# Attention beside a feed-forward network on one core: one feed-forward pair moved to between the value products and the second key tile's scores

## The chip, the cores and the metric

The kernel runs on one core of a Trainium2 chip. The metric is the device time of one execution in microseconds (us); less is better. TensorE (PE in the profile) multiplies matrices and writes to eight banks of accumulators (PSUM); its weight loads are listed apart as PEld. VectorE (DVE), ScalarE (ACT) and GpSimd (POOL) do the rest, and SyncE (SP) issues most transfers. The engines run side by side and wait for each other through semaphores.

## The reference

```python
xn = _layernorm(x)                          # x: [1, 2048, 512]
q, k, v = split(xn @ wqkv)                  # 32 heads of 16
p = _softmax(q @ k^T * 16 ** -0.5)          # full, over 2048 keys
s = (p @ v) @ wo
h = _silu(xn @ w_gate) * (xn @ w_up)        # 1792 hidden features
g = _silu(h @ w_down)
return x + s * g
```

All inputs are float32. One block of 2048 tokens goes through attention with 32 small heads and, beside it, through a gated feed-forward network; the second's result gates the first's.

## The kernel before

The kernel has a prologue of some 160 us (normalising, transposing, projecting to queries, keys and values, which go to memory in the layout that attention reads), an attention loop, and a short end for the last token block.

**Attention.** The heads are taken in 8 groups of 4 and the tokens in 4 query blocks of 512, which gives 32 units (`u`). Each unit runs over the 2048 keys in 8 steps of two key tiles of 128 (`kp`, and `i` = 0 or 1 in it), 256 steps in all. For a key tile TensorE makes four score matrices of 128 keys x 512 queries, one a head (line 811). The heads of a group sit in the two halves of the array's rows, so two of these matmuls form a pair and run beside each other. A pair fills one of two score tiles (`score[0]`, `score[1]`, `j` = 0 or 1) of two accumulator banks each, and one ScalarE instruction of 1024 columns takes the exponential of it into SBUF (line 813). Both key tiles of a step use the same two score tiles, so each pair of scores has to wait until the exponential of the pair two before it has read its tile.

Between the first and the second key tile's scores stand the value products of the step before (`values(prev)`, line 356): 16 matmuls of 17 columns (16 values and a column of ones that gives the sum), four beside each other in four strips of the array's columns. The order of a step on TensorE is thus: scores of key tile 0, value products of the previous step, scores of key tile 1, feed-forward work.

**Feed-forward work.** The network's matmuls, and the output projection behind them, are written as generators (`ffn`, `project_out`). Each `next` of one issues a pair: two matmuls that take the two halves of the contraction in the two halves of the array's rows, into `bankx` and `banky` (`both`, line 174). The precision of float32 is kept by splitting operands into a high and a low part, three products for each. A tile of the up projection (128 of the 1792 gate and up features for 512 tokens) has 24 pairs; a tile of the down projection has 24 or 18. When a tile's last pair is issued, ScalarE and VectorE empty the two banks; until then both belong to that tile. The generator yields the number of pairs that its tile still lacks, which the kernel before doesn't use. Some instructions hang on a pair's number: behind the 8th pair of an up-projection tile its down weights are fetched, behind the last one the tanh, the products and the splitting of the hidden features follow.

**Who gets how many.** `plan` writes the list `shares`, one entry a step: an up-projection tile is spread over three steps of 8 pairs, a down-projection tile of 24 over three of 8 or, every eighth, two of 12, one of 18 over two of 9, an output-projection tile is one step. `share()` at a step's end, behind the second key tile's scores, takes the next entry and calls `fill(n)`, which draws n pairs. The first steps are given some pairs by hand (`FIRST`). TensorE takes everything in the order in which it is written.

Of the kernel before, what the change touches and what calls it, by code (L numbers as in the profile page):

```python
# [50 lines left out]
def tile_block(ctx: ExitStack, tc: tile.TileContext, x, wqkv, wo, w_gate, w_up, w_down, out):  # L51
# [51 lines left out]
    def load_k(g, c, i=None):  # L103
        load_rows(kst[(g * NB + c) % RING if i is None else i],
                  k_d[:, g * 64:(g + 1) * 64, c * TB:(c + 1) * TB], KSLOT)

    def load_q(u, i=None):
        g, b = divmod(u, NB)
        load_rows(qst[u % 2 if i is None else i], q_d[:, g * 64:(g + 1) * 64, b * TB:(b + 1) * TB], QSLOT)

    def load_shift(u):
        for h in range(2):
            sp.dma_start(qst[u % 2][h * HALF:h * HALF + 2].bitcast(F32),
                         sh_d.rearrange("(s u) (j h t) -> u h s j t", s=2, j=2, h=2)[u, h])

    def load_v(g, c):
        sp.dma_start(vst[(g * NB + c) % RING], v_d[g][:, c * CT:(c + 1) * CT])
# [38 lines left out]
    def catch_up():  # L156
        while after:
            after.pop(0)()
# [131 lines left out]
    def out_steps():  # L290
        for b in range(NB - 1):
            if b not in stage and (len(queue) <= NB, 0 in stage and now > stage.get(0, now), ready[0] == DT)[b]:
                for c in range(DT - 1):
                    load_out(b, c)
                stage[b] = now
            if b in stage and b < 2 and (b, 1) not in stage and now > (u0 + b) * steps:
                load_out(b, DT - 1)
                stage[b, 1] = now
            if b in stage and (b, 2) not in stage and now > stage[b] and (b < 2 or len(queue) <= 2):
                splits.extend((b, c) for c in range(DT - 1))  # L300
                stage[b, 2] = now
                for t in range(0 if b else NT):
                    load_gates(t)
            if (b, 1) in stage and (b, 5) not in stage and now > stage[b, 1]:
                splits.insert(0 if not b else len(splits), (b, DT - 1))
                stage[b, 5] = now
        for _ in range(min(2, len(splits))):
            b, c = splits.pop(0)
            split_o(lhs[b, c], parts_o[b, c])
            ready[b] += 1  # L310
# [27 lines left out]
    def load_gate():  # L338
        last.extend(on[:3] + [one.tile([P, D], F32, tag="wdr", name="last")])
        for t in range(NT):  # L340
            r = rows[(NB - 1) * NT + t]
            sp.dma_start(gate[t], g_d[r])
            sp.dma_start(last[t], x[r])

    def gate_rest(t):
        dve.scalar_tensor_tensor(facc[:, t], facc[:, t], 0.5, gate[t], op0=ALU.mult, op1=ALU.mult)
        dve.tensor_add(facc[:, t], facc[:, t], last[t])


    def values(item):  # L350
        u, kp, probs = item
        v, a = vst[(u // NB * NB + kp * 2 // CT) % RING], acc[u % 2]
        for i in range(2):
            kt = 2 * kp + i
            for h in range(4):
                mm(a[h * 32:h * 32 + DH + 1], v[:, kt % CT, h * (DH + 1):(h + 1) * (DH + 1)],  # L356
                   probs[2 * i + h // 2][:, h % 2], start=kt == 0, stop=kt == KT - 1, skip_group_check=True)
# [35 lines left out]
    queue = [[None, ffn(b), NF * 3 * (DC + NT)] for b in range(NB)]  # L393
    queue += [[None, project_out(NB - 1, DT - 1), EARLY * 3 * (DT - 1)]]
    queue += [[b, project_out(b), NT * 3 * DT] for b in range(NB - 1)]
    total = sum(q[2] for q in queue)
    given = 0

    now = -1

    def fill(n):
        nonlocal given
        while n > 0 and not blocked():
            next(queue[0][1])
            queue[0][2] -= 1
            if not queue[0][2]:
                queue.pop(0)
            n -= 1
            given += 1
# [3 lines left out]
    shares = []  # L413
# [24 lines left out]
    def blocked():  # L438
        return not queue or queue[0][0] is not None and ready[queue[0][0]] < DT

    def share():
        if not blocked() and shares:
            fill(shares.pop(0))


    with ExitStack() as pro:
# [211 lines left out]
        for b in range(NB):  # L658
# [3 lines left out]
            for n, (make, i) in enumerate(slots):  # L662
# [56 lines left out]
                if not more and n == 9:  # L719
                    tops = pps.tile([P, 512], F32, tag="ps", name="tops")  # L720
                    nc.tensor.transpose(tops[0:1, :P], sm, ident)
                    dve.reduce_max(s4, tops[0:1, :P], axis=AX.X)
                    dve.tensor_scalar(s4, s4, 0.51, None, op0=ALU.mult)
                    dve.tensor_scalar(flag, s4, LIMIT, None, op0=ALU.is_le)
                    dve.tensor_scalar(sel[:, :NG * NB], row[:, :NG * NB], s4, None, op0=ALU.mult)
                    for h in range(2):
                        dve.tensor_copy(selq[:, h * HALF:h * HALF + 1], s4)
                    fill(3 * DC)
                    low, high = [pps.tile([P, 512], F32, tag="ps", name="low") for _ in range(2)]
                    mm(high[:2 * NG * NB, :8], sel, row[:, :8], start=True, stop=True, skip_group_check=True)  # L730
                    mm(low[:HALF + 2, :8], selq, row[:, :8], start=True, stop=True, skip_group_check=True)
                    act(shift, high[:2 * NG * NB, 0:1].to_broadcast([2 * NG * NB, 512]), AF.Copy, scale=-1.0)
                    for h in range(2):
                        two_rows = slice(h * HALF, h * HALF + 2)
                        act(qst[0][two_rows], low[two_rows, None, 0:1].to_broadcast([2, 2, 512]), AF.Copy, scale=-1.0)
                    for j in range(4):
                        pool.dma_start(sh_d[:, j * 512:(j + 1) * 512], shift.bitcast(F32))
                    fast = nc.values_load(flag, min_val=0, max_val=1)
# [58 lines left out]
    for u in range(units):  # L797
        g, b = divmod(u, NB)
        q = qst[u % 2]
        for kp in range(steps):  # L800
            now = u * steps + kp
            probs = []
            for i in range(2):
                kt = 2 * kp + i
                k, kc = kst[(g * NB + kt // CT) % RING], kt % CT
                if now == i == 0:
                    fill(FIRST[0])
                for j in range(2):
                    for h in range(2):
                        r = slice(h * HALF, h * HALF + NROW)  # L810
                        mm(score[j][:, h], k[r, j, kc * P:(kc + 1) * P], q[r, j], start=True, stop=True)  # L811
                    pr = ppool.tile([P, 2, TB], F32, tag="pr", name="pr")
                    exps.append(act(pr, score[j], AF.Exp, scale=0.25))  # L813
                    if i == 0 and j == 1 and now:
                        tc.add_manual_dep(exps[-1].ins, exps[-3].ins.name, settled, reason="order of the slots' writes")
                    probs.append(pr)
                    if now == i == 0 and j:
                        fill(FIRST[1])
                    elif (now, i, j) in ((0, 1, 0), (1, 0, 0)):
                        fill(FIRST[2 + now])  # L820
                if i == 0:
                    catch_up()
                if i == 0 and prev:
                    values(prev)
            old, prev = prev, (u, kp, probs)
            share()
            if old and old[1] == steps - 1:
                after.append(partial(finish, old[0]))
            if kp == 0:
                if u + 1 < units:  # L830
                    load_q(u + 1)
                    load_shift(u + 1)
            if g + 1 < NG and (b == 0 and kp == 0 or b == NB - 1 and kp in (2, 4, 6)):
                load_k(g + 1, kp // 2)
                load_v(g + 1, kp // 2)
            out_steps()
            if now == (units - 1) * steps + 1:
                load_gate()
            if 0 <= now - (units - 1) * steps - 4 < EARLY:
                gate_rest(now - (units - 1) * steps - 4)  # L840
# [79 lines left out]
```

## Time and profile before

| | before |
|---|---|
| time of 3 runs: median (lowest to highest) | 1437.24 us (1437.2 to 1437.76) |
| span of the profiled execution, first to last instruction | 1435.2 us |
| granted TensorE clock, mean | 1.000 |
| busy between 200 and 1200 us of the span (1000 us): TensorE, ScalarE, VectorE | 1000.0, 825.9, 337.1 us |
| DMA share of its engines between 200 and 400 us | 0.26 |

The timed runs include what lies around the span; the median is 2.0 us above it. A row of the profile reads: line of the code, engine, operation, what it writes <- what it reads, shape, how often, then busy time and mean duration, then the idle time of the engine ahead of it and who ended that. A row of the timeline begins with its start and its length in us, and "x2" means that two like instructions are merged in it. Two matmuls in different halves of the rows run beside each other and start within some nanoseconds, so a pair is one place in TensorE's time.

### The profile page before, as it was taken

To read this page: it belongs to the slowest core of one execution; us is meant where nothing else is said; L and a number is where in the kernel's file an instruction comes from. 1 tells how busy PE (TensorE), PEld (TensorE's weight loads), DVE (VectorE), ACT (ScalarE), POOL (GpSimd) and SP (SyncE) were. 2 spreads that over 40 slices of the span, in tenths; PEclk is the share of its full clock that TensorE was granted. 3 is DMA by queue.
4 is the path that set the end of the run, shared out by engine and by line. 5 is a ranking of instruction groups with operands and counts; after the bars stand their busy time and mean duration, and the time that the engine had idled before them with its cause. 6 is when DMAs were issued, how large, how long until landed. Compare 5 with 4: busy or idle time off the path is not lost.

```text
span 1435.2 us, 26816 instructions
## 1 busy us (share of the span) xinstructions
PE 1427.3 (99%) x11227; PEld 804.0 (56%) x11227; DVE 537.9 (37%) x899; ACT 1111.2 (77%) x1235; POOL 90.9 (6%) x104
## 2 busy tenths in 40 slices
PE   9999999999999999999999999999999999999998
PEld 7778655555555555555555555555555555555555
DVE  6543344112523343134323441243244422243665
ACT  6733688888888888778888888888888887888764
POOL 4200200000000000000000000000000000000154
PEclk9999999999999999999999999999999999999999
DMA  7778652032264321142553320342835210312553
GB/s 222 264 246 248 160 116 63 19 90 65 67 149 120 96 65 34 39 105 71 112 132 90 95 48 12 79 106 55 177 79 123 63 42 12 101 30 78 196 183 104
DMA packets 127524, 149.15 MB, mean 104 GB/s; under 512 B 12588, under 2 KB 79404, under 8 KB 126628
## 3 DMA queue, kind: packets, MB, share of 16 engines
q1 hardware_dynamic: 122196, 126.84, 34.5%
q0 software_dynamic: 4912, 20.12, 3.8%
q8 instruction: 91, 1.49, 0.5%
q10 hardware_dynamic: 288, 0.39, 0.1%
q14 instruction: 37, 0.30, 0.1%
HBM read 107.20 MB, written 40.11 MB: 103 GB/s over the span
## 4 chain that ended last, share of the span: by engine, by line
PE 89%; DVE 0%; DVEq 0%; issue 0%
PE acc L356 33%; PE bankx L174 31%; PE score L811 20%; PE banky L174 3%; PE acc L858 0%; PE banky L858 0%; PE score L858 0%; DVE y L865 0%; DVE y L871 0%; DVEq L916 0%
## 5 line engine op out<-in xcount | busy, mean ns | idle before, releaser
L813 ACT ACTIVATE pr<-score 128x1024 f32<-128x1024 f32 x1024 | 993.2, 1023 | 223.2 <-PE score L811 222.5
L356 PE MATMUL acc<-pr,vst 128*17 128x512 f32 x4096 | 489.2, 595 | 0.0
L811 PE MATMUL score<-qst,kst 50*128 50x512 f32 x2048 | 352.3, 421 | 0.0
L811 PEld LDWEIGHTS score<-qst,kst 50*128 50x128 f32 x2048 | 177.2, 184 | 263.8 <-ACT pr L813 227.9
L174 PE MATMUL bankx<-fx,guh 64*128 64x512 f32 x896 | 288.8, 392 | 0.1
L174 PE MATMUL banky<-fx,guh 64*128 64x512 f32 x896 | 288.7, 392 | 0.0
L356 PEld LDWEIGHTS acc<-pr,vst 128*17 128x17 f32 x4096 | 93.9, 96 | 234.4 <-issue 233.6
L204 DVE SCALAR_TENSOR_TENSOR ga<-th,bankx 128x512 f32<-128x512 f32 x56 | 38.5, 687 | 446.1 <-ACT th L203 446.1
L174 PEld LDWEIGHTS bankx<-fx,guh 64*128 64x128 f32 x896 | 165.7, 185 | 32.8 <-issue 0.9
L174 PE MATMUL banky<-fx,gul 64*128 64x512 f32 x448 | 175.3, 391 | 0.0
L174 PE MATMUL bankx<-fx,gul 64*128 64x512 f32 x448 | 175.3, 391 | 0.0
L174 PEld LDWEIGHTS banky<-fx,guh 64*128 64x128 f32 x896 | 165.6, 185 | 4.0
L174 PE MATMUL bankx<-wd,hh 64*128 64x512 f32 x672 | 166.7, 389 | 0.0
L174 PE MATMUL banky<-wd,hh 64*128 64x512 f32 x672 | 166.6, 388 | 0.0
L174 PEld LDWEIGHTS bankx<-wd,hh 64*128 64x128 f32 x672 | 124.0, 185 | 26.6
L174 PEld LDWEIGHTS banky<-wd,hh 64*128 64x128 f32 x672 | 124.0, 185 | 1.2
L174 PEld LDWEIGHTS bankx<-fx,gul 64*128 64x128 f32 x448 | 82.8, 185 | 17.0
L174 PEld LDWEIGHTS banky<-fx,gul 64*128 64x128 f32 x448 | 82.8, 185 | 2.0
L569 PE MATMUL ps<-xt,wh 128*128 128x512 f32 x256 | 80.6, 396 | 0.0
L222 DVE COPY facc<-bankx 128x512 f32<-128x512 f32 x16 | 11.1, 691 | 171.5 <-PE banky L174 171.5
L135 DVE TENSOR_TENSOR gul<-gur,guh 128x1024 fp32r<-128x1024 f32 x56 | 68.6, 1225 | 2.4 <-DVE guh L134 0.5
L379 POOL DMA_DIRECT2D o_d<-o x12 | 6.5, 545 | 756.5 <-DVE o L377 563.8
(158 smaller groups left out, 1060.5 us busy)
## 6 DMA issues: line engine op xcount, KB each, us to landing
gur<-in_B_w_gate_dram SPq DMA_DIRECT2D x56, 256.0 KB
gur<-in_B_w_up_dram SPq DMA_DIRECT2D x56, 256.0 KB
wdr<-in_B_w_down_dram SPq DMA_DIRECT2D x56, 256.0 KB
kst<-k_d SPq DMA_DIRECT2D x192, 64.0 KB
qst<-q_d SPq DMA_DIRECT2D x192, 64.0 KB
fx<-xt_d SPq DMA_DIRECT2D x24, 512.0 KB
q_d<-parts SPq DMA_DIRECT2D x16, 512.0 KB
k_d<-parts SPq DMA_DIRECT2D x16, 512.0 KB
```

The lines of the kernel that those rows point to most:

```text
L135: dve.tensor_sub(lo, raw, hi.bitcast(F32))
L174: mm(bank, lhs[h], rhs[h], start=start, stop=stop)
L204: dve.scalar_tensor_tensor(ga, th, 1.0, bankx, op0=ALU.add, op1=ALU.mult)
L222: dve.tensor_copy(facc[:, t], bankx)
L356: mm(a[h * 32:h * 32 + DH + 1], v[:, kt % CT, h * (DH + 1):(h + 1) * (DH + 1)], probs[2 * i + h // 2][:, h % 2], start=kt == 0, stop=kt == ...
L379: (pool if g < NG - 1 else sp).dma_start(o_d[g // 2, b], o2)
L569: mm(ps, w, a[:, c], start=n == 0, stop=n == 3 * DT - 1)
L811: mm(score[j][:, h], k[r, j, kc * P:(kc + 1) * P], q[r, j], start=True, stop=True)
L813: exps.append(act(pr, score[j], AF.Exp, scale=0.25))
```

## The change

`fill` keeps what the generator yields, in `left`: the number of pairs that the tile under way still lacks, 0 when a tile is complete. In the step loop, right behind the value products and so ahead of the second key tile's scores, one pair is drawn if a tile is under way and the step's share has more than one; the share is lessened by one, so the step issues as many pairs as before.

```diff
-    given = 0
+    given = left = 0
...
     def fill(n):
-        nonlocal given
+        nonlocal given, left
         while n > 0 and not blocked():
-            next(queue[0][1])
+            left = next(queue[0][1])
             queue[0][2] -= 1
...
                 if i == 0 and prev:
                     values(prev)
+                    if left and shares and shares[0] > 1:
+                        fill(1)
+                        shares[0] -= 1
             old, prev = prev, (u, kp, probs)
             share()
```

## The prediction

> **What bounds the kernel now.** I read the page first, for what sets the end, and then one step of the attention loop instruction by instruction, since the change sits inside a step.
>
> ```profile
> span 1435.2 us, 26816 instructions
> ...
> PE 1427.3 (99%) x11227; PEld 804.0 (56%) x11227; DVE 537.9 (37%) x899; ACT 1111.2 (77%) x1235; POOL 90.9 (6%) x104
> ...
> PE acc L356 33%; PE bankx L174 31%; PE score L811 20%; PE banky L174 3%; PE acc L858 0%; PE banky L858 0%; PE score L858 0%; DVE y L865 0%; DVE y L871 0%; DVEq L916 0%
> ...
> L813 ACT ACTIVATE pr<-score 128x1024 f32<-128x1024 f32 x1024 | 993.2, 1023 | 223.2 <-PE score L811 222.5
> ...
> L811 PEld LDWEIGHTS score<-qst,kst 50*128 50x128 f32 x2048 | 177.2, 184 | 263.8 <-ACT pr L813 227.9
> ```
>
> TensorE (PE) is busy all the time and carries the chain of waits: value products (L356), feed-forward pairs (L174), scores (L811). But the last two rows say that it is a loop of two engines: exponentials wait for scores, and the weight loads of scores wait for exponentials. A busy PE row can hide a wait, so the question is how much room that second wait has. There are 1024/4 = 256 steps. I take one that ends inside a feed-forward tile, from the timeline cut into narrow windows. PE first (start, length, instruction):
>
> ```profile
> 461.99 0.63 PE L811 MATMUL score<-qst,kst 50*128 50x512 f32 x4
> 462.56 1.91 PE L356 MATMUL acc<-pr,vst 128*17 128x512 f32 x16
> 463.86 0.61 PE L356 MATMUL acc<-pr,vst 128*17 128x512 f32 x4
> 464.40 0.50 PE L811 MATMUL score<-qst,kst 50*128 50x512 f32 x2
> 464.74 0.39 PE L811 MATMUL score<-qst,kst 50*128 50x512 f32 x2
> 464.97 0.39 PE L174 MATMUL bankx<-fx,gul 64*128 64x512 f32 x1
> 465.20 0.39 PE L174 MATMUL bankx<-fx,guh 64*128 64x512 f32 x1
> ...
> 466.83 0.40 PE L811 MATMUL score<-qst,kst 50*128 50x512 f32 x2
> 467.06 0.39 PE L811 MATMUL score<-qst,kst 50*128 50x512 f32 x2
> ```
>
> The step is 466.83 - 461.99 = 4.84 us: first key tile's scores (two pairs, call them A0 and A1), 16 value matmuls, second key tile's scores (B0 at 464.40, B1 at 464.74), eight feed-forward pairs 0.23 apart (464.97 to 465.20), then the next step's A0 and A1. Now ScalarE and the score loads in the same step:
>
> ```profile
> 462.43 1.03 ACT L813 ACTIVATE pr<-score 128x1024 f32<-128x1024 f32 x1 [0.42 <-PE score L811]
> 464.94 1.02 ACT L813 ACTIVATE pr<-score 128x1024 f32<-128x1024 f32 x1 [0.57 <-PE score L811]
> 465.87 1.02 ACT L813 ACTIVATE pr<-score 128x1024 f32<-128x1024 f32 x1
> ```
>
> ```profile
> 464.40 0.19 PEld L811 LDWEIGHTS score<-qst,kst 50*128 50x128 f32 x2 [0.85 <-ACT pr L813]
> 466.60 0.19 PEld L811 LDWEIGHTS score<-qst,kst 50*128 50x128 f32 x2
> 466.93 0.19 PEld L811 LDWEIGHTS score<-qst,kst 50*128 50x128 f32 x2
> ```
>
> The reader is to see one thing here. The exponential of B1 runs from 465.87 to 466.89, and the weight load of the next A1, which will write the same score banks, starts at 466.93, 0.04 later. It was held: A0's load came with the last pair at 466.60, 0.23 ahead of its matmul, while A1's comes 0.13 ahead of its own at 467.06. A load that isn't hidden costs 0.34 - 0.23 = 0.11 (B0 at 464.40 to B1 at 464.74, against the pair spacing). So A1 starts on time with 0.13 - 0.11 = 0.02 us to spare. **The exponentials of the second key tile have no room left in a step with eight pairs.**
>
> The same near the end of the run:
>
> ```profile
> 1295.35 1.02 ACT L813 ACTIVATE pr<-score 128x1024 f32<-128x1024 f32 x1
> 1296.42 0.19 PEld L811 LDWEIGHTS score<-qst,kst 50*128 50x128 f32 x2
> ```
>
> In a down-projection step:
>
> ```profile
> 880.69 1.02 ACT L813 ACTIVATE pr<-score 128x1024 f32<-128x1024 f32 x1
> 881.63 0.40 PE L811 MATMUL score<-qst,kst 50*128 50x512 f32 x2
> 881.76 0.18 PEld L811 LDWEIGHTS score<-qst,kst 50*128 50x128 f32 x2 [0.17 <-ACT pr L813]
> ```
>
> And in a step with nine pairs:
>
> ```profile
> 719.96 1.02 ACT L813 ACTIVATE pr<-score 128x1024 f32<-128x1024 f32 x1
> 721.13 0.41 PE L811 MATMUL score<-qst,kst 50*128 50x512 f32 x2
> 721.13 0.21 PEld L811 LDWEIGHTS score<-qst,kst 50*128 50x128 f32 x2
> ```
>
> Held until 1296.42, 0.05 after the exponential's end at 1296.37; held until 881.76, 0.13 after A0's matmul, nothing to spare. With nine pairs the exponential ends at 720.98 and the load goes with A0 at 721.13, free since about 721.03.
>
> **The change part by part.** No instruction is added or removed. Keeping the yielded count is done while the program is built and issues nothing. In a step whose feed-forward tile is already begun, one pair (two loads, two matmuls) goes from behind B1 to ahead of B0. Which pairs: the tiles of the up projection with 24 pairs in three steps of 8 give their 9th and 17th; the down-projection tiles likewise, or the 13th of 24 or 10th of 18 where they take two steps. The loads, tanh and bank copies in that code hang on pairs 8 and 24 or the last, so no transfer is moved past SP's or POOL's queue, and no bank is emptied earlier or later within the tile.
>
> How many steps, from the planner: 56 up-projection tiles, of which the first is made ahead of the loop, the second takes two steps (1 moved pair), 54 take three (108). Of the 16 tiles in the longer down-projection group 14 take three steps (28), 2 take two steps of twelve (2); 16 of the shorter group take two of nine (16). The output projection's tiles take one step each and give none. In all 155 pairs, 137 of them in steps of about eight.
>
> *PE's own work: nothing.* The pair leaves a place where it cost 0.23. In front it stands where B0 stands, pays the 0.34 that B0 paid (464.40 to 464.74), and B0 then costs 0.23. Before the trace has a pair right behind value products this is unseen, so I bound it. The switch from value products to scores now costs 0.11 + 0.11: value groups start 0.43 apart (below), the last one 0.54 ahead of B0's load, and then the load lies open.
>
> ```profile
> 462.55 0.13 PEld L356 LDWEIGHTS acc<-pr,vst 128*17 128x17 f32 x8 [0.30 <-issue]
> 463.43 0.12 PEld L356 LDWEIGHTS acc<-pr,vst 128*17 128x17 f32 x4 [0.31 <-issue]
> ```
>
> At best a pair escapes both, a gain of 0.22; at worst B0 pays an open load again behind it, a loss of 0.11. I take 0: the pair has the shape 64x128 against B0's 50x128, both in the two row halves, and they follow each other at 0.23 in the row pair 464.74 and 464.97. That B0's load waits for an exponential is not what holds it: the one it needs ended at 463.46, 0.94 earlier. The Trainium skill, page "TensorEngine Tiling (Array Packing)", section Key Properties, says that a change of tiling mode drains the engine; the extra 0.11 behind the last value group agrees.
>
> *The exponentials of B0 and B1: each 0.23 later.* B0's matmul really starts at 464.40 + 0.11 = 464.51 now, and at 464.74 behind the pair. ScalarE has nothing else to do there (idle 0.57 for B0's score), so the exponential of B1 ends at 466.89 + 0.23 = 467.12. PE, with its work unchanged, still reaches A0 at 466.83. A1's load starts at 467.16, its matmul can run from 467.27 in place of 467.06: **0.21 us of stall.** PE works in order, so the value products, B0, B1 and all pairs behind A1 wait with it. What is late next: everything in that step moves by 0.21, its end too, so relative to the next A0 the exponentials stand as before and the next step pays the same 0.21 if it has a moved pair, and nothing if not. A0 itself is not held: its exponential ends at 465.96 + 0.23, its load is at 466.60. Nor are the first tile's exponentials: the first starts 0.44 after A0 (461.99 to 462.43), so at 467.27 in the next step, and finds ScalarE free, since exponentials follow each other by 0.93 (464.94 to 465.87) and B1's then starts at 466.10.
>
> Sum: 109 up-projection steps at 0.21 = 22.9; 28 down-projection steps at 0.23 (no room to spare) = 6.4; 16 steps of nine pairs: 720.98 + 0.23 + 0.04 + 0.11 = 721.36 against A1 due at 721.13 + 0.23 = 721.36, nothing, hidden by the ninth pair; 2 of twelve, nothing. Together 29.3.
>
> *One saving.* The step after an up-projection tile has a tanh ahead of its exponentials, and there B1 waits:
>
> ```profile
> 457.32 0.60 ACT L203 ACTIVATE th<-bankx 128x512 f32<-128x512 f32 x1 [0.15 <-PE banky L174]
> 458.71 1.03 ACT L813 ACTIVATE pr<-score 128x1024 f32<-128x1024 f32 x1
> 459.52 0.19 PEld L811 LDWEIGHTS score<-qst,kst 50*128 50x128 f32 x2 [0.85 <-ACT pr L813]
> 459.80 0.19 PEld L811 LDWEIGHTS score<-qst,kst 50*128 50x128 f32 x2
> 460.13 0.39 PE L174 MATMUL bankx<-fx,guh 64*128 64x512 f32 x1
> ```
>
> B0's load to the first pair is 0.61 here against 0.57 (464.40 to 464.97): 0.04 lost. This step begins a tile, so no pair is moved in it; but it follows a moved one, so its value products end 0.21 later while the tanh, waiting on PE, does not. B1's load then meets a finished exponential: 54 x 0.04 = 2.2 back. Net 29.3 - 2.2 = 27.1. The span goes from 1435.2 to 1462.3; the median of the timed runs, 1437.24, lies 2.0 above the span, so **1464.3 us**, 1.9% slower. This case's own range, with 0.17 to 0.25 for the 137 stalls and the saving or not, is 1458 to 1472.
>
> **The rivals.** *The pair goes in for free* (the other side). If the pair's loads are made under the value products and PE doesn't empty, each moved step gains up to 0.22: 155 x 0.22 = 34, and the stalls stay (the exponentials follow A0 at the same distance, whichever moves): 1437.2 + 27 - 34 = 1430. It is not slower from 27.1/155 = 0.175 of the 0.22 on. Against it: the value loads at 462.55 carry no wait of the trace, and PE's loader stood 0.30 ahead of them with nothing but the switch to wait for. Half of it, the load hidden and the emptying paid, gives 0.11 x 155 = 17 less: 1447. Beside this stands the Trainium skill, page "TensorE: Matmul & The Clock Gate", section Step-by-step: weight loads are pulled ahead of running matmuls when their row groups don't conflict or they go to the background buffer. By that rule 1447 is the answer; the two quoted switches don't show it.
>
> *Paid twice.* B0 behind the pair pays an open load of its own, 0.11 x 155 = 17, and its exponential is late by that too, a further 0.11 on 137 steps = 15: at most 1464 + 32 = 1496, 1481 without the second. Only the equal spacing of 464.74 and 464.97 speaks against it.
>
> *No stall, or no move.* If A1 could run beside a late exponential, or the condition held nowhere, the time stays at 1437. The load rows that start 0.04 to 0.05 after an exponential's end, at 466, 881 and 1296, speak against the first, the planner's shares of 8 against the second.
>
> **How the numbers follow.** Forecast 0.83 (1464.3); load hidden 0.05 (1447); free 0.03 (1430); paid twice 0.05 (1481 to 1496); no stall or no move 0.04 (1437). A measurement of this kernel tells 0.2%, about 3 us, from no change. Faster 0.03, same 0.04, slower 0.93. The range 1449 to 1474 holds the forecast's own and a little of the neighbours.
>
> **What would show it.** Right: in a moved step one L174 pair starts where B0's load started, B0 0.34 behind it; the exponential of B1 ends about 0.29 after the next A0 starts in place of 0.06; A1's load 0.05 behind that; A0 to the first value product 0.77 in place of 0.57; steps of eight pairs 5.05 long after a moved step and 4.84 else; idle of the score loads by exponentials up by some 25 us; nine-pair steps as long as before. Wrong: A1's load not behind an exponential, the pair behind the value products starting less than 0.5 after the last group, or B0 more than 0.4 behind the pair.

## The result, and the profile after

| | before | after |
|---|---|---|
| time of 5 runs: median (lowest to highest) | 1437.41 us (1437.2 to 1437.76) | 1464.11 us (1463.95 to 1464.49) |
| span of the profiled execution | 1435.2 us | 1462.2 us |

The change makes the kernel slower: ratio 1.0186, 95% interval 1.0174 to 1.0198. The forecast was 1464.3 us. The page of the changed kernel, as far as it answers to the rows shown of before:

```profile
span 1462.2 us, 26816 instructions
...
PE 1454.6 (99%) x11227; PEld 804.3 (55%) x11227; DVE 538.1 (37%) x899; ACT 1106.2 (76%) x1235; POOL 90.9 (6%) x104
...
L813 ACT ACTIVATE pr<-score 128x1024 f32<-128x1024 f32 x1024 | 993.2, 1023 | 262.7 <-PE score L811 256.7
```

The instructions are as many as before, and TensorE still shows 99%: its busy time has grown by 27.3 us, about as much as the span (27.0). That is no added work. A matmul's row is 0.39 us long although pairs follow each other at 0.23, and one whose weights come late is listed longer still (0.51 at 474.29 below), so the rows overlap and a wait of 0.21 leaves no gap between them. Of these rows only ScalarE's, with 34 us more idle time for scores, shows that the loop has slowed down. The wait itself has to be looked for in one step. This is the counterpart of the step in the prediction, from the timeline of TensorE in narrow windows (start, length, instruction):

```profile
469.11 0.39 PE L811 MATMUL score<-qst,kst 50*128 50x512 f32 x2
...
470.97 0.61 PE L356 MATMUL acc<-pr,vst 128*17 128x512 f32 x4
471.51 0.50 PE L174 MATMUL bankx<-fx,gul 64*128 64x512 f32 x1
...
471.85 0.40 PE L811 MATMUL score<-qst,kst 50*128 50x512 f32 x2
472.09 0.39 PE L811 MATMUL score<-qst,kst 50*128 50x512 f32 x2
472.32 0.39 PE L174 MATMUL bankx<-fx,guh 64*128 64x512 f32 x1
...
473.95 0.39 PE L811 MATMUL score<-qst,kst 50*128 50x512 f32 x2
474.29 0.51 PE L811 MATMUL score<-qst,kst 50*128 50x512 f32 x2
474.73 0.62 PE L356 MATMUL acc<-pr,vst 128*17 128x512 f32 x4
...
479.00 0.39 PE L811 MATMUL score<-qst,kst 50*128 50x512 f32 x2
```

The exponentials of this step, from ScalarE's timeline, and the weight loads of the moved pair and of the next A1, from the loader's:

```profile
472.29 1.03 ACT L813 ACTIVATE pr<-score 128x1024 f32<-128x1024 f32 x1 [0.81 <-PE score L811]
473.21 1.02 ACT L813 ACTIVATE pr<-score 128x1024 f32<-128x1024 f32 x1
```

```profile
471.51 0.18 PEld L174 LDWEIGHTS bankx<-fx,gul 64*128 64x128 f32 x1 [0.85 <-issue]
...
474.29 0.19 PEld L811 LDWEIGHTS score<-qst,kst 50*128 50x128 f32 x2 [0.38 <-ACT pr L813]
```

The reader is to see four things. The moved pair stands at 471.51, 0.54 behind the last value group, where B0 stood; B0 follows 0.34 later, B1 another 0.24, so TensorE's own order costs what it cost. The step is still 473.95 - 469.11 = 4.84 us. The exponential of B1 now ends at 474.23, 0.28 behind the next A0 (0.06 before), and the load of A1 starts at 474.29, 0.06 behind that end. From that A0 to the first value product it is 0.78 us (0.57 before), and the step that pays is 479.00 - 473.95 = 5.05 long. The loss of a moved step thus shows in the step behind it. The trace has the same in all 137 steps that stand behind a moved step of eight pairs: the load of A1 starts 0.05 us behind the exponential's end (0.050 to 0.053), and that end lies 0.29 behind A0 in the median, where it was 0.06.

### The profile page after: what moved, and what is told of

Read it like the earlier page. It is cut to its first block, busy times and chain, and to the rows that moved or that the text cites. A ratio compares the mean times of both kernels' runs of the same rounds, so it can differ in the third digit from the quotient of the medians.

```text
span 1462.2 us, 26816 instructions
## 1 busy us (share of the span) xinstructions
PE 1454.6 (99%) x11227; PEld 804.3 (55%) x11227; DVE 538.1 (37%) x899; ACT 1106.2 (76%) x1235; POOL 90.9 (6%) x104
## 4 chain that ended last, share of the span: by engine, by line
PE 89%; DVE 0%; DVEq 0%; issue 0%
PE bankx L174 32%; PE acc L356 32%; PE score L811 20%; PE banky L174 4%; PE acc L861 0%; PE banky L861 0%; PE score L861 0%; DVE y L868 0%; DVE y L874 0%; DVEq L919 0%
## 5 line engine op out<-in xcount | busy, mean ns | idle before, releaser
L811 PE MATMUL score<-qst,kst 50*128 50x512 f32 x2048 | 362.8, 416 | 0.0
L174 PE MATMUL bankx<-fx,guh 64*128 64x512 f32 x896 | 294.2, 398 | 0.1
L174 PE MATMUL banky<-fx,guh 64*128 64x512 f32 x896 | 294.2, 398 | 0.0
L811 PEld LDWEIGHTS score<-qst,kst 50*128 50x128 f32 x2048 | 185.8, 185 | 169.9 <-ACT pr L813 145.3
L174 PEld LDWEIGHTS bankx<-fx,guh 64*128 64x128 f32 x896 | 165.5, 185 | 78.7 <-issue 47.7
L174 PE MATMUL bankx<-fx,gul 64*128 64x512 f32 x448 | 181.1, 404 | 0.0
L174 PE MATMUL banky<-fx,gul 64*128 64x512 f32 x448 | 181.0, 404 | 0.0
L174 PE MATMUL banky<-wd,hh 64*128 64x512 f32 x672 | 178.8, 396 | 0.0
L174 PE MATMUL bankx<-wd,hh 64*128 64x512 f32 x672 | 178.8, 396 | 0.0
L174 PEld LDWEIGHTS banky<-fx,guh 64*128 64x128 f32 x896 | 165.5, 185 | 5.2
L174 PEld LDWEIGHTS bankx<-wd,hh 64*128 64x128 f32 x672 | 123.9, 184 | 63.5 <-issue 39.1
L174 PEld LDWEIGHTS banky<-wd,hh 64*128 64x128 f32 x672 | 123.9, 184 | 1.2
L174 PEld LDWEIGHTS bankx<-fx,gul 64*128 64x128 f32 x448 | 82.5, 184 | 60.4 <-issue 45.9
L174 PEld LDWEIGHTS banky<-fx,gul 64*128 64x128 f32 x448 | 82.6, 184 | 2.3
```

The source lines that it names most:

```text
L174: mm(bank, lhs[h], rhs[h], start=start, stop=stop)
```

## The experiments

All ratios are to the kernel before, timed on the same chip. The theory under test: the second key tile's exponentials come 0.23 us later, and the next A1's weight load is held by them. Its main rivals: the place behind the value products costs something on TensorE itself, or any moved pair does.

| run | median, us | ratio (95% interval) |
|---|---|---|
| ahead_of_values | 1464.36 | 1.0187 (1.017 to 1.0204) |
| between_b0_b1 | 1437.93 | 1.0003 (0.9993 to 1.0012) |
| two_pairs | 1499.11 | 1.0428 (1.0411 to 1.0445) |
| between_a0_a1 | 1450.49 | 1.0095 (1.0078 to 1.0112) |
| long_steps | 1437.78 | 1.0 (0.9991 to 1.0009) |
| b0_b1_all | 1436.25 | 0.999 (0.9981 to 0.9999) |
| short_before | 1435.6 | 0.9986 (0.9977 to 0.9996) |
| short_after | 1434.91 | 0.9979 (0.997 to 0.9989) |

**Another place with the same delay.** Against the changed kernel:

```diff
                 if i == 0 and prev:
-                    values(prev)
                     if left and shares and shares[0] > 1:
                         fill(1)
                         shares[0] -= 1
+                    values(prev)
```

> The moved pair stands between the first key tile's scores and the value products instead of behind the value products, in the same steps. Theory (the exponentials of the second key tile come 0.23 us later, and the next A1's weight load is held by them): B0 and B1 are as late as in the changed kernel, so about 1464 us, 1.019 of before. Rival (what costs is the place behind the value products, the switch of the array's columns into a feed-forward pair): the pair now follows scores at 0.23 us, so 1437 us.

1464.36 us. The pair no longer stands behind the value products, and the cost is the same. In its trace, too, the load of A1 starts 0.05 us behind the late exponential in those 137 steps. The place isn't what costs.

**Another place without the delay.** The three lines go into the loop over the score pairs, behind the exponential's issue:

```diff
                     probs.append(pr)
+                    if i == 1 and j == 0 and prev and left and shares and shares[0] > 1:
+                        fill(1)
+                        shares[0] -= 1
```

> The moved pair stands between B0 and B1, the two score pairs of the second key tile, in the same 155 steps. Theory: ScalarE takes B0's exponential first and reaches B1's 0.93 us later, while B1's scores have been ready for 0.46 us; 0.23 us of delay to B1 alone reaches no exponential, so about 1437 us, 1.000 of before. Rival (each pair taken out of the stretch between B1 and the next A1 shortens the cover by 0.23 us, or each moved pair costs its 0.2 us): 1464 us.

1437.93 us: no difference. As many pairs are moved, in the same steps, past one score pair in place of two, and the 27 us are gone. TensorE, ScalarE and the loader in such a step (first three rows, next two, last):

```profile
464.71 0.50 PE L811 MATMUL score<-qst,kst 50*128 50x512 f32 x2
465.05 0.40 PE L174 MATMUL bankx<-fx,gul 64*128 64x512 f32 x1
...
465.28 0.41 PE L811 MATMUL score<-qst,kst 50*128 50x512 f32 x2
```

```profile
465.25 1.02 ACT L813 ACTIVATE pr<-score 128x1024 f32<-128x1024 f32 x1 [0.57 <-PE score L811]
466.18 1.02 ACT L813 ACTIVATE pr<-score 128x1024 f32<-128x1024 f32 x1
```

```profile
467.25 0.19 PEld L811 LDWEIGHTS score<-qst,kst 50*128 50x128 f32 x2
```

B1 comes 0.57 behind B0 (465.28 - 464.71) in place of 0.34. Its exponential starts at 466.18 all the same, 0.93 behind B0's, because ScalarE has B0's to do first. B1 would have been ready at 465.72 (its start and the 0.44 that lie between a score pair and its exponential), so 0.46 is left to spare. The exponential ends at 467.20 and the load of A1 starts at 467.25, as in the kernel before. What has to be kept early is B0, not the whole second key tile. The rival that counts the pairs between B1 and the next A1 falls here: those are seven in this kernel too.

**Twice the dose.** Against the changed kernel:

```diff
-                    if left and shares and shares[0] > 1:
-                        fill(1)
-                        shares[0] -= 1
+                    if left and shares and shares[0] > 2:
+                        fill(2)
+                        shares[0] -= 2
```

> Two pairs instead of one behind the value products, in the same steps. Theory: the exponentials come 0.46 us later, each of the 137 steps of about eight pairs stalls by 0.44 instead of 0.21, and the 16 nine-pair steps, which had just room for one pair, stall by 0.23: 1464 + 137 x 0.23 + 16 x 0.23 = about 1499 us. Rival (a price for breaking the order at this place once a step): 1464 us.

1499.11 us. The second pair costs 35.0 us where the first cost 26.7, as the used-up room asks: the first pair still had 0.02 us of it in an up-projection step, and the nine-pair steps took the first pair for nothing and not the second. The traces agree step by step: against the changed kernel, the 137 steps behind a moved step of eight pairs are 0.23 us longer, and the 16 behind a nine-pair step are 0.23 us longer too.

**Ahead of the first key tile's second scores.** As in between_b0_b1, with another condition:

```diff
                     probs.append(pr)
+                    if i == 0 and j == 0 and prev and left and shares and shares[0] > 1:
+                        fill(1)
+                        shares[0] -= 1
```

> The moved pair stands between A0 and A1, the two score pairs of the first key tile, in the same steps (second and third of a tile). Theory: what counts is the number of pairs from B1 to the next A1, of which eight just cover. From a tile's first to its second step there are nine, from the second to the third eight, from the third to the next tile's first seven, so one stall a tile instead of two: 54 x 0.21 + 14 x 0.23 = 14.6, less the 2.2 of the tanh steps: about 1450 us. Rivals: each moved pair costs: 1464 us; only the place behind the value products costs: 1437 us.

1450.49 us, half of the loss. B0 is late here as in the changed kernel, in two steps of each tile. But a pair between A0 and A1 also makes the next A1 due 0.23 later, and that covers the step between the two; only the step at the tile's end, behind which no pair stands ahead of A1, pays. The traces show it: against the kernel before, the third steps of the 54 up-projection tiles are 0.01 us longer, the 55 steps that follow an up-projection tile 0.16. Neither "each moved pair costs" (1464) nor "the place costs" (1437) gives this. The expectation counts pairs from B1; after between_b0_b1 the count is rather from B0 to the next A1, which is the same number here.

**Only where there is room.** Against the changed kernel:

```diff
-                    if left and shares and shares[0] > 1:
+                    if left and shares and shares[0] > 8:
```

> The pair behind the value products is drawn in the steps of nine and twelve pairs alone, 18 of the 155. Theory: their exponentials have 0.13 us and more to the next A1 over what the stretch needs, so nothing is held beyond its cover: 1437.4 us, 1.000 of before. Rival (each moved pair costs 27/137 = 0.2 us wherever it is): 18 x 0.2 = 3.5 us more, 1441 us.

1437.78 us, beside 1437.72 of before on the same chip. Its interval ends at 1.0009, 1.3 us; the rival's 3.5 us lie outside. A pair behind the value products is free in a step of nine or twelve in this kernel.

**The cause taken away.** If late exponentials are all of it, shorter ones must make the change free. Both kernels get these edits, with six fixed tiles in place of the rotating ones so that the columns left out are defined:

```diff
+SHORT = 384
...
-    ppool = ctx.enter_context(tc.tile_pool(name="ppool", bufs=6))
+    ppool = ctx.enter_context(tc.tile_pool(name="ppool", bufs=1))
+    prs = [ppool.tile([P, 2, TB], F32, name=f"pr{i}") for i in range(6)]
+    for i in prs:
+        pool.memset(i, 1.0)
...
-                    pr = ppool.tile([P, 2, TB], F32, tag="pr", name="pr")
-                    exps.append(act(pr, score[j], AF.Exp, scale=0.25))
+                    pr = prs[len(exps) % 6]
+                    exps.append(act(pr[:, :, :SHORT], score[j][:, :, :SHORT], AF.Exp, scale=0.25))
...
-    spare, *y = [ppool.tile([P, 2, TB], F32, tag="pr", name="y") for _ in range(3)]
+    spare, *y = prs[:3]
```

> Each exponential takes 384 of the 512 columns of each of its two banks; a quarter of the exponentials is left out, and the value products read what stands there from the start. Theory: an exponential takes some 0.25 us less, the score loads are never held in a step of eight pairs, and only the 2.2 us of the tanh steps go: about 1435 us. Rival: the same.

> The same with a quarter of the exponentials left out, with the pair behind the value products as in the changed kernel. Theory (the change costs only through late exponentials): with 0.5 us of room the 0.23 us reach nothing, so the time of the kernel with short exponentials and the old order, about 1435 us. Rival (the order on TensorE itself costs): 27 us more than that, 1462 us; half of each: between.

1435.6 us with the old order and 1434.91 us with the moved pair. The order that cost 27 us costs nothing once an exponential lasts 0.81 us in place of 1.02. A moved step of short_after, ScalarE, TensorE and the loader:

```profile
465.41 0.81 ACT L817 ACTIVATE pr<-score 128x768 f32<-128x768 f32 x1
```

```profile
466.36 0.39 PE L815 MATMUL score<-qst,kst 50*128 50x512 f32 x2
```

```profile
466.36 0.19 PEld L815 LDWEIGHTS score<-qst,kst 50*128 50x128 f32 x2
```

The exponential of B1 ends at 466.22, 0.14 ahead of the next A0 at 466.36, and A1's load goes with A0: nothing is held. The expectations had 0.25 us less for an exponential and 0.5 us of room. The rows give 0.21 less, and a room of 0.14 and the 0.23 that the pair has taken, 0.37 in all, which is still enough.

The same two kernels show how far the view of waits can be trusted. These are its rows for the loader, of short_before, of the kernel before, of the changed kernel (two rows), in that order (idle time in us, times, longest):

```profile
PEld score L815 <- ACT pr L817: 217.2, 256, 0.9
```

```profile
PEld score L811 <- ACT pr L813: 227.9, 320, 0.9
```

```profile
PEld score L811 <- ACT pr L813: 145.3, 283, 0.9
PEld bankx L174 <- issue: 132.7, 157, 0.9
```

In short_before no score load of a step of eight pairs is held, yet 217.2 us stand there: 0.85 once in each of the 256 steps. That is the loader's idle time across the last value products, which ends with B0's load and is put down to ScalarE because that load carries a wait, long over. So 217 of the 227.9 us of before were no wait for ScalarE either. In the changed kernel the moved pair ends that idle time in 155 steps, and 155 x 0.85 = 132 us go over to "issue"; 101 x 0.85 = 86 are left under the scores (short_after, where nothing is held, has 85.3 there, 101 times). The other 59 us stand ahead of loads that are truly held.

**A pair between B0 and B1 in every step.** As between_b0_b1, in each step that has more than one pair, a tile's first step among them:

```diff
                     probs.append(pr)
+                    if i == 1 and j == 0 and prev and not blocked() and shares and shares[0] > 1:
+                        fill(1)
+                        shares[0] -= 1
```

> One pair of every step with more than one, also of a tile's first step, stands between B0 and B1. Theory: as with the second and third steps nothing is late, and in the 54 steps that follow an up-projection tile, where B1's load waits 0.04 us for the exponential that the tanh made late, the pair fills that wait: 54 x 0.04 = 2.2 us less than before, 1435.2 us, 0.9985 of before. Rival (a new tile's first pair, now 0.24 us earlier, waits for the banks, or the delay of B1 reaches the next A1): over 1437 us.

1436.25 us against 1437.72, ratio 0.999 (0.9981 to 0.9999): 1.5 us less, two thirds of the 2.2 expected, and the interval only just leaves out no change. The trace is clearer than the total: the 55 steps that follow an up-projection tile are 0.045 us shorter than before, 2.5 us together. All other steps together are 1.0 us longer, and why stays open. The step after an up-projection tile, with its tanh, shows the mechanism (ScalarE, the loader, TensorE):

```profile
458.69 1.03 ACT L813 ACTIVATE pr<-score 128x1024 f32<-128x1024 f32 x1
```

```profile
459.82 0.19 PEld L811 LDWEIGHTS score<-qst,kst 50*128 50x128 f32 x2
```

```profile
459.49 0.49 PE L811 MATMUL score<-qst,kst 50*128 50x512 f32 x2
459.82 0.39 PE L174 MATMUL bankx<-fx,guh 64*128 64x512 f32 x1
...
460.05 0.39 PE L811 MATMUL score<-qst,kst 50*128 50x512 f32 x2
```

The exponential that B1 waits for ends at 459.72. B1's load now goes with the pair ahead of it at 459.82 and isn't held (in the kernel before it came 0.06 after that end and cost 0.04), B1 follows 0.23 behind the pair, and the new tile's first pair starts in its turn, 0.33 behind B0, so the banks were empty in time.

## Why the prediction was right, by its steps

**No room in a step of eight pairs.** Right, and the step that carried the sum. That A1's load starts 0.04 to 0.05 behind an exponential although nothing is lost yet was the sign of it. short_after and long_steps show the other side: with room the same move is free.

**TensorE's own work unchanged.** Right: 0.54 and 0.34 at the switch as before. ahead_of_values, where the pair stands in another place, costs the same. The rivals "goes in for free", "load hidden" and "paid twice" are out. Beside "load hidden" the prediction set a rule of the Trainium skill, page "TensorE: Matmul & The Clock Gate", section Step-by-step: weight loads are pulled ahead of running matmuls when their row groups don't conflict or they go to the background buffer. Its first condition isn't met here, as the value products take all 128 rows of the array (128*17 in the profile); whether a load could go to the background buffer no run shows. The moved pair's load had an idle loader ahead of it for 0.85 us and started only with the pair itself, at 471.51.

**0.21 us a step.** Right: A0 to the value products went from 0.57 to 0.78. **Which steps pay.** Right, when each step (from A0 to the next A0) is compared in the two traces. The third steps of the 54 up-projection tiles are 0.21 us longer each; the 28 steps behind a moved down-projection step of eight pairs 0.23; the 18 behind a step of nine or twelve 0.00. long_steps shows the 18 by themselves, and in two_pairs the 16 behind a nine-pair step start to pay. **The sum.** 27.1 foreseen, 27.0 measured in the spans (1462.2 - 1435.2).

**The saving of 2.2 us in the tanh steps.** Right. The total can't tell it apart, but the steps can: the 55 steps that follow an up-projection tile are 0.165 us longer than before, 0.046 less than the 54 third steps, 2.5 us together. So the forecast's sum holds term by term and not by errors that cancel. That this wait can be filled is shown by the same 55 steps of b0_b1_all, too.

**What was wrong** is one of the signs that the prediction named. It said that the score loads' idle time put down to exponentials would rise by some 25 us; it fell by 82.6 (227.9 to 145.3). I had read the page's row as a wait of the loop. Most of it was the gap across the value products, as the short exponentials show, and the move gave that gap to another row. The forecast didn't suffer, because its terms came from the load's start against the exponential's end in single steps.

**What the prediction didn't see:** that delaying B1 alone is free. It named the two exponentials together; ScalarE's order makes B0 the one that counts, and B1 had 0.69 us to spare in the step of the prediction (464.74 + 0.44 against 465.87), of which the pair takes 0.23.

## What to carry to other kernels

Where two engines feed each other through two buffers, an engine that shows 99% may still be at the edge of a wait; compare when a held load or matmul starts with when its releaser ends, and count the room in single steps before moving anything ahead of the work that the other engine waits for. Here a moved pair cost nothing in itself: what cost was the dependent work that it made late, and the same move one place further on, behind the first of two buffers, was free. A row of waits in the profile can name a semaphore that was long over, as 217 of the 227.9 us did here.

## What was not expected of the hardware

A weight load for which the profile shows no wait isn't begun during value products that use four column strips, though the loader is idle: 0.85 us in each of the 155 moved steps (155 of the 157 times in the row "PEld bankx L174 <- issue" above). And overlapping rows hide most of the waiting even in two_pairs, whose span is 62.5 us (1497.7 - 1435.2) above that of before: TensorE still shows 98%.

```profile
PE 1464.9 (98%) x11227; PEld 804.9 (54%) x11227; DVE 538.0 (36%) x899; ACT 1098.5 (73%) x1235; POOL 90.9 (6%) x104
```
